# Sparse attention and feed-forward in exact fp32: series and weight conversion in PSUM, chunks of four tiles, the first chunk's strips split around the second chunk

## The chip, the cores and the metric

The kernel runs on one core of a Trainium2 chip. The metric is the time of one execution on the device in microseconds (us), as the median of several runs. The engines are called as in the profile: PE (TensorE matmul), PEld (its weight loads), DVE (VectorE), ACT (ScalarE), POOL (GpSimd), SP (SyncE, which issues the DMAs).

## The reference

Attention over 4 batches of 8 heads, 768 positions, head size 64, with a block mask, and then a feed-forward layer on its output:

```python
scores = scale * q @ k.T                      # (4, 8, 768, 768), blocks of 32
mask = |blk_i - blk_j| <= 1 | first or last block row or column | 3 sampled blocks per row
attn = softmax(where(mask, scores, -1e9));  x = (attn @ v) as 3072 tokens x 512
h = x @ w_in          # 512 -> 2048
g = h - tanh(h)
out = g @ w_out       # 2048 -> 512, fp32
```

`w_in` and `w_out` are float64. q, k, v and the output are fp32.

## The kernel before

**Attention** works on 16 pairs of heads and writes x to DRAM (`xscr`). The change leaves it alone, but for its last rows, which already belong to the feed-forward part.

**Feed-forward** works on tiles of 128 tokens (24 tiles) and on strips of 128 of the 2048 hidden features (16 strips, counted by `ft`). A chunk is a group of tiles that goes through all 16 strips; `CHUNKS` gives chunks of 6 (worked as two halves of 3), 4, 4, 4, 4 and 2 tiles. One step is one strip for one chunk or half:

- `first` (L503): 12 matmuls make `h` of the strip, in a PSUM bank from a pool of two (`one`). Every fp32 product is three matmuls (high by high, high by low, low by high part), over four blocks of 128 features of x.
- The series, which makes `g` = h − tanh(h): ACT makes `u` = h² (L510), `t` = tanh h (L512) and `qq` (L514); POOL a mask `mk` (L516); DVE multiplies out a polynomial for small h in `g` (L518, L520, L521), makes t − h (L519) and copies that over `g` under the mask (L522). All of them but `h` lie in SBUF. Then ACT makes the high part `gh` (L525) and POOL the low part `gl` (L526).
- `second` (L539, L540, L541): three matmuls for each tile add the strip's share to the tile's output bank. Six banks in three tiles of two banks (`big`, named o0, o1, o2) are output banks. After strip 15 they are copied out, by DVE (L545) or ACT (L547), and written by DMA.

`second` of a step is issued two steps after its `first` (`LAG`), so that its series has that long. Where 4 tiles are worked, the next chunk's x is loaded at strip 5 and turned (4 transposes for each tile, L426, into banks 4 and 5, that is tile o2; ACT L428 makes the high part, DVE L429 the low part) from strip 10.

**The weights** come as float64 words. `load_w` brings half a megabyte into one of four `stage` buffers (L400, L404), `convert` makes fp32 from it by three integer operations of DVE (L411, L414, L417, all in SBUF), ACT splits off the high part (L472) and POOL the low part (L474). The six conversions of strips 0 to 2 are done during attention and kept in DRAM; the other 26 lie in the first chunk, two ahead of each strip.

**The order** on each engine is set by a scheduler from the program's order and from the dependencies. It keeps dependencies by tile: two views of one tile, such as the two banks of o2, count as the same, where one of them is written.

Of the kernel before, what the change touches and what calls it, by code (L numbers as in the profile page):

```python
# [406 lines left out]
def convert(nc, pool, raw, name):  # L407

    w = raw.rearrange("p (n w) -> p n w", w=2)
    t = pool.tile([P, 512], I32, tag="wcvt", name=name)  # L410
    nc.vector.tensor_scalar(  # L411
        out=t, in0=w[:, :, 1], scalar1=3, scalar2=0x3FFFFFF8, op0=ALU.logical_shift_left, op1=ALU.bitwise_and
    )
    nc.vector.scalar_tensor_tensor(  # L414
        out=t, in0=w[:, :, 1], scalar=-0x40000000, in1=t, op0=ALU.bitwise_and, op1=ALU.bitwise_or
    )
    nc.vector.scalar_tensor_tensor(  # L417
        out=t, in0=w[:, :, 0], scalar=29, in1=t, op0=ALU.logical_shift_right, op1=ALU.bitwise_or
    )
# [16 lines left out]

class FFN:
    LAG = 2

    def __init__(self, tc, w_in, w_out, xscr, ident, qbias, ps, slots, wt, out, f2):  # L440
        self.nc = tc.nc
        self.tc = tc
        self.w_in, self.w_out, self.xscr, self.ident, self.qbias, self.wt, self.out, self.f2 = (
            w_in, w_out, xscr, ident, qbias, wt, out, f2
        )
# [8 lines left out]
        self.pend = []
        self.raw = {}

    def fetch_w(self, ft):
        nc, tiles, wi, wo, wt = self.nc, self.tiles, self.wi, self.wo, self.wt
        for x, m in enumerate("io"):
            hi, lo = tiles.pop(0), tiles.pop(0)  # L460
            (wi, wo)[x][0][ft], (wi, wo)[x][1][ft] = hi, lo
            if ft < NPRE:
                nc.sync.dma_start(out=lo.bitcast(F32), in_=wt[m, ft])
            else:
                load_w(nc, self.stage[(2 * ft + x) % 4], self.w_in, self.w_out, m, ft)

    def split_w(self, ft):
        nc, wi, wo = self.nc, self.wi, self.wo
        for x, m in enumerate("io"):
            hi, lo = (wi, wo)[x][0][ft], (wi, wo)[x][1][ft]  # L470
            t = lo.bitcast(F32) if ft < NPRE else convert(nc, self.f2, self.stage[(2 * ft + x) % 4], f"cvt{m}{ft}")
            nc.scalar.activation(out=hi, in_=t, func=AF.Copy)  # L472
            eng = nc.vector if ft < 2 and x else nc.gpsimd
            eng.tensor_tensor(out=lo, in0=t, in1=hi.bitcast(F32), op=ALU.subtract)  # L474

    def fetch_x(self, n, j):

        if n == 1:
            raw = self.f2.tile([P, DM], F32, tag="wcvt", name=f"xn{n}_{j}")
        else:  # L480
            raw = self.xbuf[0].bitcast(F32)[:, 4096 + 512 * j : 4096 + 512 * (j + 1)]
        b, t = divmod(self.start[n] + j, T)
# [9 lines left out]
    def first(self, n, s, ft):  # L492
        nc, wi, f2 = self.nc, self.wi, self.f2
        xh, xl = x_parts(self.xbuf[n % 2], sum(CHUNKS[n]))
        t0, nt = sum(CHUNKS[n][:s]), CHUNKS[n][s]
# [4 lines left out]
        for c in range(NCT):  # L500
            cc = slice(c * P, (c + 1) * P)
            for w, x in ((wi[0][ft], xh), (wi[0][ft], xl), (wi[1][ft], xh)):
                nc.tensor.matmul(ph, lhsT=w[:, cc], rhs=x[:, c, tk], start=(k == 0), stop=(k == 3 * NCT - 1))  # L503
# [6 lines left out]
        nc.scalar.activation(out=u, in_=ph, func=AF.Square)  # L510
# [1 line left out]
        nc.scalar.activation(out=t, in_=ph, func=AF.Tanh)  # L512
# [5 lines left out]
        nc.vector.tensor_tensor(out=g, in0=ph, in1=u, op=ALU.mult)  # L518
        nc.vector.tensor_tensor(out=t, in0=t, in1=ph, op=ALU.subtract)  # L519
        nc.vector.scalar_tensor_tensor(out=g, in0=u, scalar=CR, in1=g, op0=ALU.subtract, op1=ALU.mult)  # L520
        nc.vector.scalar_tensor_tensor(out=g, in0=qq, scalar=QC, in1=g, op0=ALU.add, op1=ALU.mult)  # L521
        nc.vector.copy_predicated(g, mk.bitcast(I32), t)  # L522
# [2 lines left out]
        nc.scalar.activation(out=gh, in_=g, func=AF.Copy)  # L525
        nc.gpsimd.tensor_tensor(out=gl, in0=g, in1=gh.bitcast(F32), op=ALU.subtract)  # L526
# [2 lines left out]
    def second(self, n, s, ft, gh, gl):
        nc, wo, f2, out = self.nc, self.wo, self.f2, self.out  # L530
        if not n and not s and not ft:
            big = [self.big(f"o{j}") for j in range(3)]
            self.banks = [x[:, c : c + 512] for x in big for c in (0, 512)]
        banks = self.banks
        t0, nt = sum(CHUNKS[n][:s]), CHUNKS[n][s]
        for j in range(nt):
# [4 lines left out]
            nc.tensor.matmul(o, lhsT=gl[:, c], rhs=wo[0][ft], start=False, stop=(ft == NFT - 1))  # L541
            if ft == NFT - 1:
                ob = f2.tile([P, DM], F32, tag="wcvt", name=f"ob{n}_{t0 + j}")
                if j % 2:
                    nc.vector.tensor_scalar(out=ob, in0=o, scalar1=-1.0, scalar2=None, op0=ALU.mult)  # L545
                else:
                    nc.scalar.activation(out=ob, in_=o, func=AF.Copy, scale=-1.0)  # L547
                b, t = divmod(self.start[n] + t0 + j, T)
                nc.sync.dma_start(out=out[b * S : (b + 1) * S, :].rearrange("(p t) d -> t p d", t=T)[t], in_=ob)

    def step(self):
        n, s, ft = self.units.pop(0)
        if s == 0:
            if n == 0 and ft + 2 < NFT and ft:
                self.split_w(ft + 2)
            if n == 0 and ft and ft + AHEAD < NFT:
                self.fetch_w(ft + AHEAD)
        nx = sum(CHUNKS[n + 1]) if n + 1 < len(CHUNKS) else 0
        if n and ft == 5:
            for j in range(nx):  # L560
                self.fetch_x(n + 1, j)
        if n and 0 <= ft - XF < nx:
            self.turn_x(n + 1, ft - XF)
        self.pend.append((n, s, ft, *self.first(n, s, ft)))
        if n == 0 and ft == NFT - 1:
            js = [j for j in range(nx) if j // 2 == s]
            for j in js:
                self.fetch_x(1, j)
# [56 lines left out]
```

## Time and profile before

| | us |
|---|---|
| Median of 3 runs | 1017.34 (1013.38 to 1064.95) |
| The profiled execution | 1016.33 |
| Its span in the trace | 1014.5 |
| PE busy | 940.8 (93%) |
| DVE busy | 790.6 (78%) |
| POOL busy | 625.4 (62%) |
| ACT busy | 579.3 (57%) |

The span is what the trace covers; 1.8 us of the execution lie around it. `h` of the first feed-forward step starts at 419.15 us, the first chunk goes on to about 608, and the chunks after it have PE busy nearly all the time. Shares of busy time are means over these stages, so the stages are read apart.

### The profile page before, as it was taken

To read this page: it belongs to the slowest core of one execution; us is meant where nothing else is said; L and a number is where in the kernel's file an instruction comes from. 1 tells how busy PE (TensorE), PEld (TensorE's weight loads), DVE (VectorE), ACT (ScalarE), POOL (GpSimd) and SP (SyncE) were. 2 spreads that over 40 slices of the span, in tenths; PEclk is the share of its full clock that TensorE was granted. 3 is DMA by queue.
4 is the path that set the end of the run, shared out by engine and by line. 5 is a ranking of instruction groups with operands and counts; after the bars stand their busy time and mean duration, and the time that the engine had idled before them with its cause. 6 is when DMAs were issued, how large, how long until landed. Compare 5 with 4: busy or idle time off the path is not lost.

```text
span 1014.5 us, 19336 instructions
## 1 busy us (share of the span) xinstructions
PE 940.8 (93%) x7456; PEld 795.6 (78%) x7456; DVE 790.6 (78%) x1194; ACT 579.3 (57%) x912; POOL 625.4 (62%) x436
## 2 busy tenths in 40 slices
PE   5877999999999999986877899999999999999997
PEld 3666888888888887875666788888888888888896
DVE  5799788888888879899999958667666755766676
ACT  1655788888888887643443445444444534444453
POOL 1555687878777878776666646455445544544553
PEclk9798999999999999999989899999999999999999
DMA  7989576667777663143322020011000100000010
GB/s 192 256 226 223 140 187 161 157 173 175 183 168 181 154 147 109 41 159 104 95 92 83 22 94 32 11 32 42 21 11 11 63 1 1 32 11 1 1 42 22
DMA packets 73548, 97.74 MB, mean 96 GB/s; under 512 B 5880, under 2 KB 63416, under 8 KB 73456
## 3 DMA queue, kind: packets, MB, share of 16 engines
q1 hardware_dynamic: 73456, 96.51, 36.1%
q8 instruction: 59, 0.97, 0.4%
q14 instruction: 33, 0.27, 0.1%
HBM read 43.59 MB, written 14.16 MB: 57 GB/s over the span
## 4 chain that ended last, share of the span: by engine, by line
PE 61%; DVE 20%; issue 6%; ACT 5%; DMA 5%; POOL 2%; SPq 1%; POOLq 0%; DVEq 0%; ACTq 0%
PE h L503 21%; PE o L539 7%; PE o L541 7%; PE o L540 7%; PE st L264 4%; PE st L265 4%; PE sm L240 4%; ACT pe L267 2%; DVE mc L241 2%; DVE g L520 2%; PE av L301 2%; PE av L300 2%; PE av L294 2%; DVE g L522 2%; DVE ph L275 1%
## 5 line engine op out<-in xcount | busy, mean ns | idle before, releaser
L279 POOL TENSOR_TENSOR pl<-pe,ph 128x768 f16<-128x768 f32 x173 | 292.0, 1705 | 117.9 <-ACT ph L277 76.7
L526 POOL TENSOR_TENSOR gl<-g,gh 128x512 fp32r<-128x512 f32 (+2 forms) x112 | 132.0, 1181 | 177.3 <-ACT gh L525 176.8
L241 DVE TENSOR_REDUCE mc<-sm 128x1 f32<-128x768 f32 x192 | 180.2, 950 | 39.5 <-PE sm L240 38.6
L516 POOL TENSOR_SCALAR mk<-u 128x512 f32<-128x512 f32 (+2 forms) x112 | 151.5, 1352 | 80.5 <-ACT u L510 42.3
L267 ACT ACTIVATE pe<-st 128x768 f32<-128x768 f32 x192 | 153.5, 803 | 72.6 <-PE st L265 63.1
L525 ACT ACTIVATE gh<-g 128x512 fp32r<-128x512 f32 (+2 forms) x112 | 63.9, 570 | 199.2 <-DVE g L522 190.1
L518 DVE TENSOR_TENSOR g<-h,u 128x512 f32<-128x512 f32 (+2 forms) x112 | 68.4, 611 | 124.5 <-ACT t L512 118.1
L264 PE MATMUL st<-slot 128*128 128x512 f32 (+1 forms) x384 | 144.6, 377 | 7.8 <-DVE mc L241 5.2
L301 PE MATMUL av<-vhl,pl 128*128 128x65 f16 x1152 | 128.6, 194 | 4.8 <-DVE pl L279 3.0
L277 ACT ACTIVATE ph<-pe 128x768 f16<-128x768 f32 x154 | 129.0, 843 | 3.5
L294 PE MATMUL av<-vhl,ph 128*128 128x65 f16 x1152 | 129.1, 195 | 0.5 <-DVE xq L313 0.5
L300 PE MATMUL av<-vhl,ph 128*128 128x64 f16 x1152 | 128.4, 196 | 0.1
L265 PE MATMUL st<-slot 89*128 89x512 f32 (+1 forms) x384 | 125.1, 346 | 2.5 <-DMA slot<-nm 2.5
L503 PE MATMUL h<-slot,wx 128*128 128x384 f32 (+1 forms) x480 | 111.8, 383 | 13.9 <-DVE t L519 13.9
L240 PE MATMUL sm<-slot 88*128 88x512 f32 (+1 forms) x384 | 113.5, 381 | 6.9 <-DMA slot<-hiq 6.3
L301 PEld LDWEIGHTS <-pl 128*128 128x128 f16 x1152 | 107.2, 99 | 15.0 <-issue 5.6
L503 PEld LDWEIGHTS h<-slot,wx 128*128 128x128 f32 x480 | 93.1, 201 | 27.5 <-DVE t L519 17.3
L294 PEld LDWEIGHTS <-ph 128*128 128x128 f16 x1152 | 107.5, 97 | 6.1 <-issue 3.3
L300 PEld LDWEIGHTS <-ph 128*128 128x128 f16 x1152 | 108.4, 98 | 2.3 <-issue 1.9
L510 ACT ACTIVATE u<-h 128x512 f32<-128x512 f32 (+2 forms) x112 | 59.9, 535 | 78.8 <-PE h L503 61.8
L539 PE MATMUL o<-wx,gh 128*128 128x512 f32 x240 | 95.8, 399 | 6.4 <-ACT gh L525 5.4
L521 DVE SCALAR_TENSOR_TENSOR g<-qq,g 128x512 f32<-128x512 f32 (+2 forms) x112 | 89.1, 795 | 8.9 <-DVE g L520 0.5
(101 smaller groups left out, 2008.5 us busy)
## 6 DMA issues: line engine op xcount, KB each, us to landing
slot<-hik SPq DMA_DIRECT2D x64, 192.0 KB
slot<-hiq SPq DMA_DIRECT2D x64, 192.0 KB
stage<-w_in SPq DMA_DIRECT2D x13, 512.0 KB
stage<-w_out SPq DMA_DIRECT2D x13, 512.0 KB
rawk<-k SPq DMA_DIRECT2D x16, 384.0 KB
rawq<-q SPq DMA_DIRECT2D x16, 384.0 KB
slot<-lok SPq DMA_DIRECT2D x32, 192.0 KB
slot<-loq SPq DMA_DIRECT2D x32, 192.0 KB
```

The costliest lines, as they stand in the source:

```text
L240: nc.tensor.matmul(pm[:, c], lhsT=sB[s][0:88, j, t * P : (t + 1) * P], rhs=sA[s][0:88, j, c], start=True, stop=True)
L241: nc.vector.tensor_reduce(out=mcs[h][:, t : t + 1], in_=pm[:, 0:S], op=ALU.max, axis=AX.X)
L264: nc.tensor.matmul(st[:, c], lhsT=sC[s][:, j, kc], rhs=sD[s][:, j, c], start=True, stop=False)
L265: nc.tensor.matmul(st[:, c], lhsT=sA[s][0:89, j, kc], rhs=sB[s][0:89, j, c], start=False, stop=True)
L267: nc.scalar.activation(out=pe, in_=st[:, 0:S], func=AF.Exp, scale=0.125)
L279: d = eng.tensor_tensor(out=pl, in0=pe, in1=ph, op=ALU.subtract)
L294: m = nc.tensor.matmul(o[:, to, :], lhsT=ph[:, c], rhs=vv[:, 0:65], start=(kt == 0 and t == 0), stop=False, skip_group_check=True)
L300: nc.tensor.matmul(o[:, to, 0:64], lhsT=ph[:, c], rhs=vv[:, 65:129], start=False, stop=False, skip_group_check=True)
L301: nc.tensor.matmul(o[:, to, :], lhsT=pl[:, c], rhs=vv[:, 0:65], start=False, stop=last, skip_group_check=True)
L503: nc.tensor.matmul(ph, lhsT=w[:, cc], rhs=x[:, c, tk], start=(k == 0), stop=(k == 3 * NCT - 1))
L516: nc.gpsimd.tensor_scalar(out=mk, in0=u, scalar1=THR2, scalar2=None, op0=ALU.is_gt)
L539: nc.tensor.matmul(o, lhsT=gh[:, c], rhs=wo[0][ft], start=(ft == 0), stop=False)
```

## The change

**The chunks** are all of four tiles. The first chunk's strips are done in two parts: strips 0 to 5, then all 16 strips of the second chunk, then strips 6 to 15 of the first (`SEGS`). The first part's sums are written to DRAM (`part`), read back, and added at the end (L559). Output takes four banks, o0 and o1; there are 96 steps, numbered 0 to 95 below in the order in which they are issued (strip 6 of the first chunk is step 22).

**The series** is kept in PSUM: DVE makes t − h in `t` (L535), then works on `h` in place (L536, L537, L538), and copies it over `t` under a mask (L539). ACT makes the mask (L533, a Relu). GpSimd only makes low parts.

**`h`** goes around in three banks `hb`: the two of `one`, and the left half of o2, which every third step takes (2, 5, 8, ...). **The right half of o2**, `xt`, takes all transposes of x and the in-between results of the weight conversion (L418, L421; L424 reads them and writes to SBUF).

**The conversions** are issued at 1.3 for each step, from step 0 to step 19 (`RATE`). The last four, of strips 14 and 15, pass through a single buffer, `stage1`. The next chunk's x is loaded at strip 8 and turned at strips 10 to 13; the second chunk's at strips 2 to 5 of the first part.

The diff, cut to its core:

```diff
-CHUNKS = ((3, 3), (4,), (4,), (4,), (4,), (2,))
+CT = 4
+SEGS = ((0, 0, 6), (1, 0, 16), (0, 6, 16), (2, 0, 16), (3, 0, 16), (4, 0, 16), (5, 0, 16))
+RATE = 1.3
+NSTAGE, FT1 = 4, 14
...
-def convert(nc, pool, raw, name):
+def convert(nc, pool, raw, name, tmp=None):
     w = raw.rearrange("p (n w) -> p n w", w=2)
     t = pool.tile([P, 512], I32, tag="wcvt", name=name)
+    tmp = t if tmp is None else tmp.bitcast(I32)
...
-        out=t, in0=w[:, :, 1], scalar=-0x40000000, in1=t, op0=ALU.bitwise_and, op1=ALU.bitwise_or
+        out=tmp, in0=w[:, :, 1], scalar=-0x40000000, in1=tmp, op0=ALU.bitwise_and, op1=ALU.bitwise_or
     )
     nc.vector.scalar_tensor_tensor(
-        out=t, in0=w[:, :, 0], scalar=29, in1=t, op0=ALU.logical_shift_right, op1=ALU.bitwise_or
+        out=t, in0=w[:, :, 0], scalar=29, in1=tmp, op0=ALU.logical_shift_right, op1=ALU.bitwise_or
     )
...
     def turn_x(self, n, j):
-        pt = self.banks[4 + j % 2] if n > 1 else self.one(f"xt{n}_{j}")
-        split_x(self.nc, self.raw.pop((n, j)), pt, xh[:, :, jc], xl[:, :, jc], self.ident)
+        split_x(self.nc, self.raw.pop((n, j)), self.xt, xh[:, :, jc], xl[:, :, jc], self.ident)
...
-        ph = self.one(f"h{n}_{s}_{ft}")[:, 0:w_]
+        h = self.hb[self.done % len(self.hb)] if self.hb else self.one(f"h{n}_{ft}")
...
-        nc.gpsimd.tensor_scalar(out=mk, in0=u, scalar1=THR2, scalar2=None, op0=ALU.is_gt)
-        g = tl("g")
-        nc.vector.tensor_tensor(out=g, in0=ph, in1=u, op=ALU.mult)
-        nc.vector.tensor_tensor(out=t, in0=t, in1=ph, op=ALU.subtract)
-        nc.vector.scalar_tensor_tensor(out=g, in0=u, scalar=CR, in1=g, op0=ALU.subtract, op1=ALU.mult)
-        nc.vector.scalar_tensor_tensor(out=g, in0=qq, scalar=QC, in1=g, op0=ALU.add, op1=ALU.mult)
-        nc.vector.copy_predicated(g, mk.bitcast(I32), t)
+        nc.scalar.activation(out=mk, in_=u, func=AF.Relu, scale=-1.0, bias=tbias)
+        nc.vector.tensor_tensor(out=t, in0=t, in1=h, op=ALU.subtract)
+        nc.vector.tensor_tensor(out=h, in0=h, in1=u, op=ALU.mult)
+        nc.vector.scalar_tensor_tensor(out=h, in0=u, scalar=CR, in1=h, op0=ALU.subtract, op1=ALU.mult)
+        nc.vector.scalar_tensor_tensor(out=h, in0=qq, scalar=QC, in1=h, op0=ALU.add, op1=ALU.mult)
+        nc.vector.copy_predicated(t, mk.bitcast(I32), h)
...
+        big = [self.big(f"o{j}") for j in range(3)]
+        self.banks = [x[:, c : c + 512] for x in big[:2] for c in (0, 512)]
+        self.xt = big[2][:, 512:]
+        self.hb = [self.one("hb0"), self.one("hb1"), big[2][:, 0:512]]
...
+        def convert_some(k, end):
+            while k < min(end, math.ceil(RATE * self.done)):
+                self.convert_w(k)
+                if k + NSTAGE < n0:
+                    self.stage_w(k + NSTAGE)
+                elif n0 <= k < n1 - 1:
+                    self.stage_w(k + 1)
+                k += 1
+            return k
```

**Where the instructions stand, DVE.** In the middle of the first chunk of before, DVE's queue mixes the conversion of one weight strip (`cvti9`, `cvto9`) into the series of the half steps (`g0_1_6` is g of chunk 0, half 1, strip 6). The conversion's results go to SBUF, the series reads `h` from banks of its own.

```order
L518 TENSOR_TENSOR g0_1_6_8421<-h0_1_6_8400,u0_1_6_8413 128x384
L519 TENSOR_TENSOR t0_1_6_8415<-t0_1_6_8415,h0_1_6_8400 128x384
L522 COPY_PREDICATED g0_0_6_8381<-mk0_0_6_8379,t0_0_6_8375 128x384
L417 SCALAR_TENSOR_TENSOR cvti9_8440<-stage2_7869,cvti9_8440 128x512
L411 TENSOR_SCALAR cvto9_8446<-stage3_7870 128x512
L520 SCALAR_TENSOR_TENSOR g0_1_6_8421<-u0_1_6_8413,g0_1_6_8421 128x384
L414 SCALAR_TENSOR_TENSOR cvto9_8446<-stage3_7870,cvto9_8446 128x512
L521 SCALAR_TENSOR_TENSOR g0_1_6_8421<-qq0_1_6_8417,g0_1_6_8421 128x384
L417 SCALAR_TENSOR_TENSOR cvto9_8446<-stage3_7870,cvto9_8446 128x512
```

In the changed kernel DVE has this in the second chunk, where `t1_5` is t of chunk 1, strip 5 (step 11, whose `h` lies in o2) and `t1_6` that of the next step:

```order
L424 SCALAR_TENSOR_TENSOR cvti10_8373<-stage2_7855,o2_7847 128x512
L535 TENSOR_TENSOR t1_5_8394<-t1_5_8394,o2_7847 128x512
L536 TENSOR_TENSOR o2_7847<-o2_7847,u1_5_8392 128x512
L535 TENSOR_TENSOR t1_6_8442<-t1_6_8442,hb0_7848 128x512
L536 TENSOR_TENSOR hb0_7848<-hb0_7848,u1_6_8440 128x512
L537 SCALAR_TENSOR_TENSOR o2_7847<-u1_5_8392,o2_7847 128x512
L537 SCALAR_TENSOR_TENSOR hb0_7848<-u1_6_8440,hb0_7848 128x512
L538 SCALAR_TENSOR_TENSOR o2_7847<-qq1_5_8396,o2_7847 128x512
L538 SCALAR_TENSOR_TENSOR hb0_7848<-qq1_6_8444,hb0_7848 128x512
L539 COPY_PREDICATED t1_5_8394<-mk1_5_8398,o2_7847 128x512
L539 COPY_PREDICATED t1_6_8442<-mk1_6_8446,hb0_7848 128x512
L418 TENSOR_SCALAR o2_7847<-stage3_7856 128x512
```

Conversions and every third step's series now name the same tile, o2, and stand in blocks: three or four conversions, then the series of two steps side by side, then conversions again. On PE, the first matmul of step 11 (it writes o2) waits for the row of `cvti10`, and `first` of the step that uses hb0 after strip 6 waits for the row before the last.

**Where the instructions stand, PE.** Before, at strips 11 and 12 of chunk 1, the transposes of chunk 2's x go into o2, which no `first` uses, between matmuls into `h`:

```order
L503 MATMUL h1_0_11_9798<-xbuf1_9100,wx20_7844 128x512 x2
L426 MATMUL o2_7920<-ident_64,slot1_78 128x128 x4
L503 MATMUL h1_0_11_9798<-xbuf1_9100,wx21_7845 128x512
L503 MATMUL h1_0_11_9798<-xbuf1_9100,wx20_7844 128x512 x2
L503 MATMUL h1_0_11_9798<-xbuf1_9100,wx21_7845 128x512
```

Now, at the end of chunk 4, the last turn of chunk 5's x, then strip 13 of chunk 4 and strip 0 of chunk 5 (`slot1`, `slot2`: x and weights of chunk 5's first strip), all in o2:

```order
L433 MATMUL o2_7847<-ident_64,slot1_80 128x128 x4
L553 MATMUL o0_7845<-wx27_7838,gh4_12_11312 128x512
L554 MATMUL o0_7845<-wx26_7837,gl4_12_11313 128x512
L554 MATMUL o1_7846<-wx26_7837,gl4_12_11313 128x512
L552 MATMUL o1_7846<-wx26_7837,gh4_12_11312 128x512
L553 MATMUL o1_7846<-wx27_7838,gh4_12_11312 128x512
L554 MATMUL o1_7846<-wx26_7837,gl4_12_11313 128x512
L520 MATMUL o2_7847<-xbuf1_7843,wx28_7839 128x512 x2
```

The rows go on so, one strip's twelve and then the next strip's:

```order
L520 MATMUL o2_7847<-xbuf1_7843,wx28_7839 128x512 x2
L520 MATMUL o2_7847<-xbuf1_7843,wx29_7840 128x512
L520 MATMUL o2_7847<-slot1_80,slot2_81 128x512 x12
L520 MATMUL hb0_7848<-slot1_80,slot2_81 128x512 x8
L552 MATMUL o0_7845<-wx30_7841,gh4_13_11359 128x512
```

The transposes and two steps' `first` stand close behind each other in one tile, without other matmuls between the two steps. Each waits for the reader of the one before: L520 of strip 13 for DVE's L436 of the turned x, and L520 of strip 0 for L539 of strip 13.

More of the change, by code (lines that the diff above doesn't have):

```diff
@@ L39 @@
 NPRE = 3
-AHEAD = 3
 W0, DW = 40, 24.7
@@ L47 @@
 PB = 8
-XF = 10
+XF = 8
 F0, DF = 12 * (NPAIR - 1) + 1, 2
@@ L80, in attention_ffn @@
     make_identity(nc, ident)
-    qbias = cst.tile([P, 1], F32, name="qbias")
-    nc.vector.memset(qbias, QB)
+    bias = [cst.tile([P, 1], F32, name=f"bias{i}") for i in range(2)]
+    for x, val in zip(bias, (QB, THR2)):
+        nc.vector.memset(x, val)
     big = ctx.enter_context(tc.tile_pool(name="ps_big", bufs=3, space=PSUM))
@@ L91, in attention_ffn @@
     wt = {(m, ft): dpool.tile([P, 512], F32, name=f"w{m}{ft}") for ft in range(NPRE) for m in "io"}
+    part = [dpool.tile([P, DM], F32, name=f"part{j}") for j in range(CT)]
     f2 = ctx.enter_context(tc.tile_pool(name="f2", bufs=2))
-    ffn = FFN(tc, w_in, w_out, xscr, ident, qbias, ps, slots, wt, out, f2)
+    ffn = FFN(tc, w_in, w_out, xscr, ident, bias, ps, slots, wt, out, f2, part)
     with ExitStack() as actx:
@@ L384, in x_first @@
         split_x(nc, raw, pt, xa[0][:, :, j * P : (j + 1) * P], xa[1][:, :, j * P : (j + 1) * P], ident)
-    for j in range(sum(CHUNKS[0])):
+    for j in range(CT):
         at(X0 + DX * j, x_first, j)
@@ L454, in __init__ @@
+        self.done = 0
         self.pend = []
         self.raw = {}
-    def fetch_w(self, ft):
[L458 to L465, printed above, removed]
@@ L467, in split_w @@
-    def split_w(self, ft):
[L468 to L474, printed above, removed]
-    def fetch_x(self, n, j):
[L478 to L482, printed above, removed]
+        self.hb = None
@@ new lines, in place, with parts @@
+    def place(self, m, ft):
+        hi, lo = self.tiles.pop(0), self.tiles.pop(0)
+        w = self.wi if m == "i" else self.wo
+        w[0][ft], w[1][ft] = hi, lo
+        return hi, lo
+    def fetch_w(self, ft):
+        for m in "io":
+            hi, lo = self.place(m, ft)
+            self.nc.sync.dma_start(out=lo.bitcast(F32), in_=self.wt[m, ft])
+    def parts(self, t, hi, lo, eng):
+        self.nc.scalar.activation(out=hi, in_=t, func=AF.Copy)
+        eng.tensor_tensor(out=lo, in0=t, in1=hi.bitcast(F32), op=ALU.subtract)
@@ new lines, in split_w, with stage_w, convert_w @@
+    def split_w(self, ft):
+        for x, w in enumerate((self.wi, self.wo)):
+            hi, lo = w[0][ft], w[1][ft]
+            self.parts(lo.bitcast(F32), hi, lo, self.nc.vector if ft < 2 and x else self.nc.gpsimd)
+    def stage_w(self, k):
+        m, ft = "io"[k % 2], NPRE + k // 2
+        self.raw[m, ft] = self.stage[k % NSTAGE] if ft < FT1 else self.stage1
+        load_w(self.nc, self.raw[m, ft], self.w_in, self.w_out, m, ft)
+    def convert_w(self, k):
+        m, ft = "io"[k % 2], NPRE + k // 2
+        hi, lo = self.place(m, ft)
+        self.parts(convert(self.nc, self.f2, self.raw.pop((m, ft)), f"cvt{m}{ft}", self.xt), hi, lo, self.nc.gpsimd)
@@ L526, in first, with second @@
-        nc.gpsimd.tensor_tensor(out=gl, in0=g, in1=gh.bitcast(F32), op=ALU.subtract)
+        nc.scalar.activation(out=gh, in_=t, func=AF.Copy)
+        nc.gpsimd.tensor_tensor(out=gl, in0=t, in1=gh.bitcast(F32), op=ALU.subtract)
         return gh, gl
[L529 to L536, printed above, removed]
+    def second(self, x, n, ft, gh, gl):
+        nc, wo, f2 = self.nc, self.wo, self.f2
+        _, f0, f1 = SEGS[x]
+        for j in range(CT):
@@ L537, in second @@
             c = slice(j * P, (j + 1) * P)
-            o = banks[t0 + j]
-            nc.tensor.matmul(o, lhsT=gh[:, c], rhs=wo[0][ft], start=(ft == 0), stop=False)
+            o = self.banks[j]
+            nc.tensor.matmul(o, lhsT=gh[:, c], rhs=wo[0][ft], start=(ft == f0), stop=False)
             nc.tensor.matmul(o, lhsT=gh[:, c], rhs=wo[1][ft], start=False, stop=False)
[L541 to L549, printed above, removed]
@@ L551, in step @@
-    def step(self):
[L552 to L568, printed above, removed]
+            nc.tensor.matmul(o, lhsT=gl[:, c], rhs=wo[0][ft], start=False, stop=(ft == f1 - 1))
@@ new lines, in second @@
+            if ft < f1 - 1:
+                continue
+            ob = f2.tile([P, DM], F32, tag="wcvt", name=f"ob{x}_{j}")
+            if f0:
+                nc.vector.scalar_tensor_tensor(
+                    out=ob, in0=o, scalar=-1.0, in1=self.spare[j].bitcast(F32), op0=ALU.mult, op1=ALU.add
+                )
+            elif j % 2:
+                nc.vector.tensor_scalar(out=ob, in0=o, scalar1=-1.0, scalar2=None, op0=ALU.mult)
+            else:
+                nc.scalar.activation(out=ob, in_=o, func=AF.Copy, scale=-1.0)
@@ new lines, in second @@
+            b, t = divmod(CT * n + j, T)
+            if f1 == NFT:
+                nc.sync.dma_start(out=self.out[b * S : (b + 1) * S, :].rearrange("(p t) d -> t p d", t=T)[t], in_=ob)
+            else:
+                nc.sync.dma_start(out=self.part[j], in_=ob)
+                nc.sync.dma_start(out=self.spare[j].bitcast(F32), in_=self.part[j])
+    def step(self):
+        x, n, ft = self.units.pop(0)
+        f0 = SEGS[x][1]
+        last = x == len(SEGS) - 1
+        nx = None if last or x == 1 else {0: 1, 2: 2}.get(x, n + 1)
+        if nx is not None and self.hb:
+            first = 2 if x == 0 else XF
+            if nx == 2:
+                if first <= ft < first + CT:
+                    self.fetch_x(nx, ft - first)
+            elif ft == first:
+                for j in range(CT):
+                    self.fetch_x(nx, j)
+            lag = 0 if x == 0 else 2
+            if 0 <= ft - first - lag < CT:
+                self.turn_x(nx, ft - first - lag)
+        self.pend.append((x, n, ft, *self.first(n, ft)))
+        self.done += 1
@@ L569, in step @@
         if len(self.pend) > self.LAG:
             self.second(*self.pend.pop(0))
-        if n == 0 and ft == NFT - 1:
-            for j in js:
-                self.turn_x(1, j)
     def rest(self, ctx):
-        wc = ctx.enter_context(self.tc.tile_pool(name="wc", bufs=1))
-        self.tiles += [wc.tile([P, 512], F32R, name=f"wx{i}") for i in range(4 * (NFT - 6))]
-        with self.tc.tile_pool(name="stage", bufs=1) as pool:
-            self.stage = [pool.tile([P, 1024], I32, name=f"stage{i}") for i in range(4)]
-            self.fetch_w(AHEAD)
-            while self.units[0][2] < NFT - 2:
+        pool = lambda name: ctx.enter_context(self.tc.tile_pool(name=name, bufs=1))
@@ new lines, in rest @@
+        wc = pool("wc")
+        self.tiles += [wc.tile([P, 512], F32R, name=f"wx{i}") for i in range(4 * (FT1 - 6))]
+        self.xbuf.append(wc.tile([P, 4096], F32R, name="xbuf1"))
+        self.stage1 = wc.tile([P, 1024], I32, name="stage1")
+        big = [self.big(f"o{j}") for j in range(3)]
+        self.banks = [x[:, c : c + 512] for x in big[:2] for c in (0, 512)]
+        self.xt = big[2][:, 512:]
+        self.hb = [self.one("hb0"), self.one("hb1"), big[2][:, 0:512]]
+        n0, n1 = 2 * (FT1 - NPRE), 2 * (NFT - NPRE)
@@ new lines, in rest @@
+        k = 0
+        def convert_some(k, end):
[7 more added lines that the diff above has]
+            return k
+        with self.tc.tile_pool(name="stage", bufs=1) as st:
+            self.stage = [st.tile([P, 1024], I32, name=f"stage{i}") for i in range(NSTAGE)]
+            for i in range(NSTAGE):
+                self.stage_w(i)
+            self.stage_w(n0)
+            while k < n0:
@@ L582, in rest @@
                 self.step()
-        xb = ctx.enter_context(self.tc.tile_pool(name="xb", bufs=1))
-        self.xbuf.append(xb.tile([P, 4096], F32R, name="xbuf1"))
+                k = convert_some(k, n0)
+        wl = pool("wl")
+        self.tiles += [wl.tile([P, 512], F32R, name=f"wy{i}") for i in range(4 * (NFT - FT1))]
         while self.units:
             self.step()
+            k = convert_some(k, n1)
         for p in self.pend:
```

43 lines of the change are left out of this document (22 added, 21 removed).

## The prediction

> **What bounds the kernel now.** I read the profile in stages, since the shares of the page mix two programs. The columns of this view are the stretch, its length, the busy time of PE, PEld, DVE, ACT and POOL (with counts), then the granted clock and the DMA share.
>
> ```profile
> 419.15:608.20 189.05, 157.00 (x765) 133.16 (x766) 171.84 (x248) 81.33 (x161) 120.15 (x92) 0.94 0.28 89
> 608.20:958.50 350.30, 350.30 (x1579) 290.06 (x1578) 228.34 (x341) 158.43 (x278) 177.96 (x127) 1.00 0.06 20
> 958.50:1014.50 56.00, 50.30 (x300) 43.25 (x298) 40.09 (x84) 25.07 (x68) 26.94 (x33) 0.99 0.08 29
> ```
>
> Attention ends at 419.15 and stays as it is. Of the rest, 350.30 us are pure PE (busy 350.30 of 350.30): nothing done for DVE or POOL there can gain. Only the first chunk, with its 26 conversions, leaves PE idle: 32 us of 189.05, with DVE at 171.84. Its waits are for DVE's reader of `h`, since there are two `h` banks (columns: us in total, times, longest):
>
> ```profile
> PE h L503 <- DVE t L519: 20.7, 11, 2.4
> ```
>
> DVE is slow there for a reason that the mean durations show:
>
> ```profile
> L521 DVE SCALAR_TENSOR_TENSOR g<-qq,g 128x384 f32<-128x384 f32 x24 | 28.6, 1192 | 0.4
> L519 DVE TENSOR_TENSOR t<-t,h 128x384 f32<-128x384 f32 x23 | 12.4, 540 | 0.0
> L518 DVE TENSOR_TENSOR g<-h,u 128x512 f32<-128x512 f32 x64 | 44.2, 691 | 109.3 <-ACT t L512 103.8 <-POOL gl L526 5.1
> L520 DVE SCALAR_TENSOR_TENSOR g<-u,g 128x512 f32<-128x512 f32 x64 | 44.6, 697 | 0.0
> ```
>
> At one size, L521 (both inputs in SBUF) takes 1192 ns, where L519 (one input in PSUM) takes 540: the first collides with GpSimd. Later, with GpSimd less loaded, the two kinds cost the same (697 and 691).
>
> **The steady step,** out of chunk 2:
>
> ```profile
> 746.18 2.88 PE L503 MATMUL h<-slot,wx 128*128 128x512 f32 x12
> 748.41 0.63 ACT L525 ACTIVATE gh<-g 128x512 fp32r<-128x512 f32 x1 [2.99 <-DVE g L522]
> 749.12 1.29 POOL L526 TENSOR_TENSOR gl<-g,gh 128x512 fp32r<-128x512 f32 x1 [2.68 <-ACT gh L525]
> 749.16 0.60 ACT L510 ACTIVATE u<-h 128x512 f32<-128x512 f32 x1
> 750.28 0.69 DVE L518 TENSOR_TENSOR g<-h,u 128x512 f32<-128x512 f32 x1 [1.90 <-ACT t L512]
> 750.89 0.68 DVE L519 TENSOR_TENSOR t<-t,h 128x512 f32<-128x512 f32 x1
> 751.48 0.69 DVE L520 SCALAR_TENSOR_TENSOR g<-u,g 128x512 f32<-128x512 f32 x1
> 752.27 0.69 DVE L521 SCALAR_TENSOR_TENSOR g<-qq,g 128x512 f32<-128x512 f32 x1
> 753.07 0.77 DVE L522 COPY_PREDICATED g<-mk,t 128x512 f32<-128x512 int32 x1
> 754.60 0.60 ACT L510 ACTIVATE u<-h 128x512 f32<-128x512 f32 x1
> 641.00:730.00 89.00, 89.00 (x405) 73.59 (x405) 57.68 (x88) 41.02 (x72) 44.40 (x32) 1.00 0.09 30
> ```
>
> A step is 754.60 − 749.16 = 5.44 us, so a `first` or a `second` of four tiles is 2.72. One chunk's 16 steps take 89.00 with its four turned tiles: (89.00 − 87.04) / 4 = 0.49 for each. On DVE operations that don't need the one before start 0.60 apart (750.28, 750.89, 751.48), dependent ones 0.79 (752.27, 753.07). From the end of `first` (746.18 + 2.72) it is 0.26 to `u` and 1.12 more to DVE. So **the series of a step in the new order** (t − h, h·u, two dependent products, the copy) ends 0.26 + 1.12 + 0.60 + 3 × 0.79 + 0.77 = 5.1 us after its `first`; run side by side with another's (ten operations), 0.26 + 1.12 + 9 × 0.60 + 0.77 = 7.5.
>
> **The change, part by part.** *PE's work*: 96 steps × 5.44 + 20 turned tiles × 0.49 = 532.0. Before, 595.35 us from 419.15 on held about the same work, so its waits, half-clock time and tail came to some 63. The forecast is the new list of these.
>
> *What is relieved, without being on the path*: POOL loses the mask; DVE's two-input operations no longer collide. For 24 steps and 26 conversions DVE needs (24 × 5 + 78) × 0.66 = 131 where it now took 171.84. ACT gains a mask of 0.6 for each step, beside 2.6 of 5.44: hidden, as ACT waits for the copy anyway. Partial sums (four tiles out and back) have ten steps until they are needed: hidden by 54 us.
>
> *What is added* is a wait that the order shows: with `h` of every third step, the conversions and the turned x in one tile, o2, `first` waits for a DVE operation that the ring of three alone would not ask for, and behind it PE's whole queue stands still.
>
> (a) **Conversion cycle.** A conversion is L418, L421 and L424; of before:
>
> ```profile
> 433.21 0.62 DVE L411 TENSOR_SCALAR cvti<-stage 128x512 int32<-128x512 int32 x1 [1.30 <-DMA stage<-w_in]
> 434.22 0.68 DVE L414 SCALAR_TENSOR_TENSOR cvti<-stage,cvti 128x512 int32<-128x512 int32 x1
> 435.63 0.68 DVE L417 SCALAR_TENSOR_TENSOR cvti<-stage,cvti 128x512 int32<-128x512 int32 x1
> 428.87 0.40 SPq L400 DMA_DIRECT2D stage<-w_in  x1
> ```
>
> `first` of step 8 can start when cvti8's last operation is done; then DVE does the series of steps 8 and 9 side by side, and `first` of step 12 waits for step 9's copy: 7.5 us with PE idle, as nothing else stands ahead of it. Then five matmul groups follow to the next o2 step. A cycle of three steps is 6 × 2.72 + 7.5 = 23.8. DVE's own 27 operations (some 18 us) with its own idle 4.1 (`first` and the way to DVE) would be 22: not the limit. Three such cycles: 22.5 us of waits. In the fourth, the last three conversions follow each other through one buffer, each with a load of 433.21 − 428.87 = 4.3 and 2.0 on DVE, 19 in a row: I take 14 us of waits in place of 7.5. Step 23 (o2) stands right behind step 20 (o2): 6.9, its copy beside another series.
>
> (b) **Start**, up to step 8. Two series have no cover (4.5 at step 2, whose `second` comes ahead of the next `first`; 7.5 at step 9), and the second chunk's x and the first conversions share the right half: some 13 more, an estimate, since before waited 32 us over this stage. 25 in all; bounds 12 and 32.
>
> (c) **Turns.** A transpose behind an o2 step waits for that step's copy, an o2 step behind a transpose for L436. By the order of PE's rows: chunk 2's turn has two uncovered places (5.1 and 6.9), chunk 3's one (6.9), chunk 4's two half covered (4.2 each), chunk 5's one of 6.9 and one of 1.3; 35.5 us. Before had none (350.30 of 350.30).
>
> (d) **Tail**: before, the last eviction starts at 1010.69 and the span ends at 1014.5, 3.8 later.
>
> ```profile
> 1010.69 0.69 DVE L545 TENSOR_SCALAR ob<-o 128x512 f32<-128x512 f32 x1 [3.62 <-PE o L541]
> ```
>
> Now the last step's four tiles end with some 0.7 of wait for `gl` and the same 3.8: 4.5.
>
> (e) **The clock.** PE's granted clock halves after gaps:
>
> ```profile
> 446.50:448.55 2.05, 0.28 (x2) 0.00 (x1) 2.05 (x5) 1.62 (x3) 1.42 (x2) 1.00 0.35 71
> 449.65:453.05 3.40, 3.40 (x12) 3.11 (x11) 3.40 (x5) 1.45 (x4) 3.40 (x3) 0.50 0.51 161
> ```
>
> 1.8 us of idle PE are followed by 3.4 us at 0.50, that is 1.7 lost where PE is the limit. There are some nine waits of 4 us and more; at 1.5 each, 13.
>
> Sum: 419.15 + 532.0 + 25 + 22.5 + 14 + 6.9 + 35.5 + 4.5 + 13 = 1072.6; with 1.8 around the span 1074.4. The profiled execution of before is 1016.33, 1.0 below the median, so I forecast **1074 us** (5.6% slower).
>
> **What no row shows: DVE writing PSUM.** From below: no operation of 512 columns starts less than 0.60 behind another; if dependent ones in PSUM did so too, the series would be 0.6 shorter, 8 us over a dozen waits: 1066. From above, 0.3 us each (what would bring 0.69 halfway to the slowest row, 1192). I take no change, the nearest row (691 for one that reads PSUM, 697 for one that doesn't). A cost of 0.3 makes the series 0.9 longer at a dozen waits (11) and a conversion cycle, with 14 such writes, 4.2 longer (17): 1103.
>
> [...]
>
> **Rivals.** (1) *The sharing costs nothing*: the waits end before PE gets there, and the relief of DVE comes through. The start takes 12, conversion cycles are DVE's 18 (1.7 over PE's 16.3, four times), the last buffer 10, the tail 4.5, two half-clock stretches 3: 419.15 + 532.0 + 12 + 6.8 + 10 + 4.5 + 3 + 1.8 = 989: faster by 2.7%. It is decided by whether a wait ends within the 5.4 us of two groups that PE could run first; the rows of the order, with an o2 step directly behind an o2 step, speak against it. [...] Chance 0.07. (2) *Waits half covered*: (c) and (e) at half and the start at 12: 1074 − 18 − 6 − 13 = 1037, on the border of 2%. Before's eleven waits of `first` were 2.4 at most, which speaks for it; that those were for banks of tiles of their own speaks against. Chance 0.20. (3) *PSUM writes are dear*: 1103, chance 0.12. (4) *The change doesn't do what it says*, for instance the mask on ACT delays `gh`: 0.6 at each uncovered wait, 8 us more, 1082; inside the forecast's own range.
>
> **Chances and range.** Forecast 0.55 (1050 to 1090), rivals 0.07, 0.20 and 0.12, the rest unforeseen. The range for 8 in 10 takes in (2) and (3): 1034 to 1104. About 2% (997 to 1038) is what can be told from no change: faster 0.07, same 0.13 (over half of (2)), slower 0.80.
>
> **What would show it.** In the changed profile: PE's waits for DVE's L539 and L424 in blocks of about 7 us every 24 us from 495 to 600; at each turn one or two gaps of 4 to 7 us with the clock at 0.50 behind; DVE's L537 near 0.69 without the stretch to 1.1; the first h of step 20 near 597 us. The forecast is wrong if PE is busy without gaps after 610, or if gaps there stay under 2 us.

## The result, and the profile after

| | us | ratio to before |
|---|---|---|
| Before, median | 1016.67 | |
| After, median of 4 runs | 1097.83 (1096.67 to 1100.53) | 1.0814 (1.0777 to 1.085) |
| After, span of the profiled execution | 1094.5 | |

The change makes the kernel 8% slower. One of before's four executions, 1064.95 us, ran in a slower state and is left out of the ratio. The stages of after, in the view of stretches (length, then busy time of PE, PEld, DVE, ACT, POOL, the granted clock, the DMA share):

```profile
419.15:619.20 200.05, 143.77 (x580) 110.23 (x578) 126.06 (x198) 83.64 (x142) 59.39 (x47) 0.86 0.26 81
619.20:1094.50 475.30, 432.61 (x1852) 352.09 (x1852) 267.04 (x401) 229.17 (x396) 97.60 (x76) 0.95 0.07 23
```

In neither stretch is an engine busy all the time. PE idles 56 us in the first and 43 in the second; before had PE idle for 32 us in its first chunk and for none at all from 608 to 958 us. DVE and POOL did get the relief (DVE 126 us, for nearly the work that took 172). The view of waits says whom PE waited for (total, times, longest):

```profile
PE o L520 <- DVE t L539: 24.5, 4, 6.8
PE hb L520 <- DVE t L539: 22.1, 4, 7.3
PE o L433 <- DVE t L539: 17.6, 4, 6.7
PE o L552 <- ACT gh L542: 12.2, 4, 5.1
```

Sixty-four us in twelve waits are for one DVE operation, the copy that ends the series (L539), each up to 7.3 us. One of them, from the timeline of PE and then of DVE, at steps 8 and 12:

```profile
503.10 2.88 PE L520 MATMUL o<-xbuf,slot 128*128 128x512 f32 x12
513.32 1.22 PE L520 MATMUL hb<-xbuf,wx 128*128 128x512 f32 x2 [7.33 <-DVE t L539]
...
507.14 0.69 DVE L535 TENSOR_TENSOR t<-t,o 128x512 f32<-128x512 f32 x1 [6.34 <-ACT t L529]
507.74 0.69 DVE L536 TENSOR_TENSOR o<-o,u 128x512 f32<-128x512 f32 x1
508.34 0.68 DVE L535 TENSOR_TENSOR t<-t,hb 128x512 f32<-128x512 f32 x1
508.94 0.69 DVE L536 TENSOR_TENSOR hb<-hb,u 128x512 f32<-128x512 f32 x1
...
512.54 0.71 DVE L539 COPY_PREDICATED t<-mk,hb 128x512 f32<-128x512 int32 x1
513.15 0.70 DVE L418 TENSOR_SCALAR o<-stage 128x512 int32<-128x512 int32 x1
```

The order of events is to be seen here. PE finishes `first` of step 8 (into o2) at 506; DVE stands idle for 6.34 us, until 507.14, since its next work is on that `h`; then it does the series of both steps side by side, ten operations 0.60 apart; and PE starts again when the tenth is done. The two engines take turns. Right behind that, PE runs at half clock:

```profile
505.99:513.32 7.33, 0.01 (x1) 0.01 (x1) 6.18 (x11) 6.34 (x12) 0.00 (x0) 0.73 0.00 0
513.32:519.50 6.18, 6.18 (x15) 4.88 (x16) 6.02 (x10) 2.32 (x4) 3.81 (x3) 0.50 0.30 87
532.85:540.18 7.33, 0.00 (x1) 0.00 (x0) 6.17 (x11) 6.33 (x12) 0.00 (x0) 0.76 0.00 0
540.18:543.40 3.22, 3.22 (x8) 2.57 (x9) 3.06 (x5) 2.35 (x4) 2.96 (x3) 0.50 0.16 18
866.57:870.79 4.22, 0.00 (x1) 0.01 (x1) 4.22 (x8) 3.27 (x7) 0.00 (x0) 1.00 0.00 0
871.10:874.50 3.40, 3.40 (x11) 2.62 (x9) 1.71 (x4) 2.39 (x5) 2.52 (x2) 0.50 0.28 79
981.66:988.46 6.80, 0.00 (x0) 0.03 (x1) 5.65 (x10) 5.81 (x11) 0.00 (x0) 0.65 0.00 0
988.46:994.00 5.54, 5.54 (x13) 4.38 (x14) 3.32 (x6) 2.29 (x5) 2.53 (x2) 0.50 0.00 0
```

Each pair is a wait and the stretch behind it. Behind a wait of 4.2 us it is 3.4 us of PE at 0.50. Behind waits of about 7 us it is between 3.2 and 6.2, and two waits of the same 7.33 us have the two ends of that range. Over the 17 half-clock stretches after 419 us PE is busy 71 us by the trace's clock records, so some 35 us are lost to the clock; in before it was 23.5 busy and 12 lost.

### The profile page after: what moved, and what is told of

Read it like the earlier page. It is cut to its first block, busy times and chain, and to the rows that moved or that the text cites. A ratio compares the mean times of both kernels' runs of the same rounds, so it can differ in the third digit from the quotient of the medians.

```text
span 1094.5 us, 18614 instructions
## 1 busy us (share of the span) xinstructions
PE 958.9 (88%) x7264; PEld 790.4 (72%) x7264; DVE 745.4 (68%) x1120; ACT 627.1 (57%) x943; POOL 460.7 (42%) x308
## 4 chain that ended last, share of the span: by engine, by line
PE 65%; DVE 17%; ACT 6%; DMA 5%; issue 4%; POOL 1%; SPq 1%; POOLq 0%; DVEq 0%; ACTq 0%
PE hb L520 15%; PE o L520 9%; PE o L552 7%; PE o L553 7%; PE o L554 7%; PE st L270 5%; PE sm L246 4%; PE st L271 4%; ACT pe L273 2%; DVE mc L247 2%; PE av L307 2%; PE av L306 2%; PE av L300 2%; DVE t L535 2%; DVE ph L281 1%
## 5 line engine op out<-in xcount | busy, mean ns | idle before, releaser
L543 POOL TENSOR_TENSOR gl<-t,gh 128x512 fp32r<-128x512 f32 x96 | 123.2, 1289 | 468.6 <-ACT gh L542 418.3
L247 DVE TENSOR_REDUCE mc<-sm 128x1 f32<-128x768 f32 x192 | 180.0, 949 | 36.4 <-PE sm L246 35.5
L542 ACT ACTIVATE gh<-t 128x512 fp32r<-128x512 f32 x96 | 60.3, 628 | 125.8 <-DVE t L539 103.1
L535 DVE TENSOR_TENSOR t<-t,o 128x512 f32<-128x512 f32 x32 | 22.0, 686 | 118.1 <-ACT t L529 118.0
L270 PEld LDWEIGHTS st<-slot 128*128 128x128 f32 x384 | 74.0, 193 | 26.9 <-ACT pe L273 7.5
L535 DVE TENSOR_TENSOR t<-t,hb 128x512 f32<-128x512 f32 x62 | 42.4, 683 | 68.9 <-ACT t L529 68.7
L552 PE MATMUL o<-wx,gh 128*128 128x512 f32 x192 | 77.2, 402 | 5.9 <-ACT gh L542 5.1
L271 PEld LDWEIGHTS st<-slot 89*128 89x128 f32 x384 | 74.5, 194 | 10.1 <-DMA slot<-nm 1.2
L553 PE MATMUL o<-wx,gh 128*128 128x512 f32 x192 | 77.0, 401 | 0.0
L527 ACT ACTIVATE u<-o 128x512 f32<-128x512 f32 x32 | 19.1, 598 | 96.7 <-PE o L520 96.6
```

The costliest lines, as they stand in the source:

```text
L247: nc.vector.tensor_reduce(out=mcs[h][:, t : t + 1], in_=pm[:, 0:S], op=ALU.max, axis=AX.X)
L270: nc.tensor.matmul(st[:, c], lhsT=sC[s][:, j, kc], rhs=sD[s][:, j, c], start=True, stop=False)
L271: nc.tensor.matmul(st[:, c], lhsT=sA[s][0:89, j, kc], rhs=sB[s][0:89, j, c], start=False, stop=True)
```

## The experiments

**1. Is it the shared tile?** o2 becomes two tiles of one bank each; nothing else changes. To make room for tiles of another size, the pool of pairs is closed after attention.

```diff
-        big = [self.big(f"o{j}") for j in range(3)]
-        self.banks = [x[:, c : c + 512] for x in big[:2] for c in (0, 512)]
-        self.xt = big[2][:, 512:]
-        self.hb = [self.one("hb0"), self.one("hb1"), big[2][:, 0:512]]
+        bk = ctx.enter_context(self.tc.tile_pool(name="ps_bank", bufs=1, space=PSUM))
+        big = [bk.tile([P, 1024], F32, name=f"o{j}") for j in range(2)]
+        self.banks = [x[:, c : c + 512] for x in big for c in (0, 512)]
+        self.xt = bk.tile([P, 512], F32, name="xt")
+        self.hb = [self.one("hb0"), self.one("hb1"), bk.tile([P, 512], F32, name="hb2")]
...
```

> The changed kernel with one edit: the two halves of o2 become two PSUM tiles of one bank each (hb2 for h, xt for transposes and conversions); all else as changed. If the waits come from the shared tile, PE's gaps of 4 to 7 us behind it go (61 us of waits at L539 and L424) with the half-clock stretches behind them (some 30): 985 to 1010 us. If the waits come from DVE's own load or from the ring of three, the time stays above 1060.

Measured: 994.61 us (989.79 to 996.75), 0.979 of before (0.9753 to 0.9827). More than 100 us go, and all that is new is that two banks which were halves of one tile are two tiles. In the view of stretches PE is busy all the time where the changed kernel had its turns, and of the twelve waits for L539 one is left:

```profile
640.00:960.00 320.00, 320.00 (x1435) 264.77 (x1434) 209.75 (x311) 177.70 (x306) 75.03 (x58) 1.00 0.06 22
...
PE hb L522 <- DVE t L541: 6.7, 1, 6.7
```

(The lines of this kernel are two further on: L541 is the changed kernel's L539.) So the shared tile is shown as the cause; DVE's load and the ring of three are not it.

**2. The output banks as tiles of their own too.**

```diff
-        big = [bk.tile([P, 1024], F32, name=f"o{j}") for j in range(2)]
-        self.banks = [x[:, c : c + 512] for x in big for c in (0, 512)]
+        bank = lambda name: bk.tile([P, 512], F32, name=name)
+        self.banks = [bank(f"o{j}") for j in range(4)]
...
```

> As the run with o2 cut in two, and the four output banks are tiles of their own too, so that the copy of one output bank no longer holds up matmuls into its neighbour at the end of a chunk. If such pairs matter only there, 5 to 10 us less than with o2 alone cut (seven segment ends, the last one some 3 us); if not, the same within 2 us.

Measured: 988.74 us (985.65 to 990.86), 0.9742 (0.9716 to 0.9768), 6 us less than run 1, as expected of pairs that matter at segment ends. The two intervals overlap by a little, so the waits say it more plainly than the time: run 1 still had 5.3 us of such waits (its row below, PE's L554 for the copy L567), and run 2 has none.

```profile
PE o L554 <- ACT ob L567: 5.3, 3, 3.1
```

This version beats both kernels, by 2.6% and 10%.

**3. The conversions back in SBUF,** o2 still shared by `h` and the transposes.

```diff
-        self.parts(convert(self.nc, self.f2, self.raw.pop((m, ft)), f"cvt{m}{ft}", self.xt), hi, lo, self.nc.gpsimd)
+        self.parts(convert(self.nc, self.f2, self.raw.pop((m, ft)), f"cvt{m}{ft}"), hi, lo, self.nc.gpsimd)
```

> The changed kernel with the in-between results of the conversions in SBUF as before (o2 still shared by h and the transposes). If the shared tile is the cause, the waits from 500 to 620 us go and those at the turns stay: 1097.8 less 35 of waits and some 15 of half clock, 1040 to 1060 us. If DVE's load is the cause, two-input operations that collide with GpSimd again make it no better: 1085 or more.

Measured: 1045.48 us (1042.76 to 1048.83), 1.0305 (1.0275 to 1.0334), inside the 1040 to 1060 expected of the shared tile. Its waits:

```profile
PE o L520 <- DVE t L539: 20.0, 5, 6.8
PE o L433 <- DVE t L539: 17.1, 4, 6.7
PE hb L520 <- DVE t L539: 6.7, 4, 2.3
```

The waits of steps in `hb0` and `hb1`, 22.1 us in the changed kernel, fall to 6.7; those of o2's own steps and of the transposes stay. From 600 us to the tail, PE's gaps of over 1 us are the seven at the turns (4.91, 6.81, 6.71, 4.22, 4.22, 1.28 and 6.80 us). So 52 us of the loss belong to the conversions in the shared tile, and the other 51, against run 1, to the turned x in it.

**4. A bank less.** `h` goes around in two banks, and o2's left half is not used at all.

```diff
-        self.hb = [self.one("hb0"), self.one("hb1"), big[2][:, 0:512]]
+        self.hb = [self.one("hb0"), self.one("hb1")]
```

> The changed kernel with h in the two single banks only; o2's left half is unused, its right half serves conversions and transposes as changed. If the shared tile is the cause, this is faster than the changed kernel though it has a bank less: a step's first then waits for the copy two steps before, which at 5.1 us against 5.44 of cover costs little in the later chunks and some 1 to 2 us a step in the first ones, 1000 to 1030 us. If the depth of the ring matters more, slower than 1098.

Measured: 996.07 us (995.28 to 999.38), 0.9823 (0.9798 to 0.9847), a little under the 1000 to 1030 expected. The third bank, as it was placed, cost 100 us; without it PE waits 13.3 us for copies:

```profile
PE hb L520 <- DVE t L539: 13.3, 4, 4.9
```

This run leaves the pool of pairs as it was, so closing it is not what helped run 1. In a tile of its own (run 1, 994.61) the third bank is worth 1.5 us, less than the intervals tell apart.

**5. Is the rest the clock?** Twenty-six matmuls that add zeros to an output bank stand behind `first` of steps 8, 11, 14, 17 and 20, to keep PE busy in five of the waits.

```diff
+KEEP, NKEEP = (8, 11, 14, 17, 20), 26
...
+        if self.done - 2 in KEEP:
+            for _ in range(NKEEP):
+                m = self.nc.tensor.matmul(self.banks[0], lhsT=self.zero, rhs=self.wi[0][0], start=False, stop=False)
+                self.tc.add_manual_dep(
+                    m.ins, self.ends[self.done - 2].ins.name,
...
```

> The changed kernel, with 26 more matmuls that add zeros to an output bank (5.9 us of PE) right behind the first of steps 8, 11, 14, 17 and 20, that is inside the waits of 5 to 7 us. The half-clock stretches behind these five waits hold 26.5 us of busy PE. If that clock is what the prediction sized too low, they go and the time falls by 10 to 13 us, to 1084 to 1088; if another thing slows the stage, it stays at 1096 to 1101, or grows.

Measured: 1088.8 us (1086.33 to 1090.65), 1.0731 (1.0706 to 1.0757): 9 us less than the changed kernel though PE does 130 matmuls more, a little under the 10 to 13. The stretches of this kernel, then one of the changed one:

```profile
514.07:520.00 5.93, 5.93 (x26) 4.91 (x27) 5.75 (x10) 2.32 (x4) 3.85 (x3) 1.00 0.27 88
489.70:598.90 109.20, 99.32 (x428) 79.22 (x426) 71.92 (x114) 47.13 (x80) 37.22 (x29) 1.00 0.24 78
```

```profile
489.70:598.90 109.20, 80.05 (x303) 63.11 (x302) 69.05 (x109) 46.67 (x79) 36.44 (x29) 0.84 0.24 73
```

In the 6 us behind the first wait PE now does 26 matmuls at clock 1.00, where the changed kernel did 15 at 0.50. The clock's share is shown for these waits; that the same holds at the turns follows from the rows above and was not tried. The gain falls short in part because this kernel has a half-clock stretch that the changed one has not, behind a wait of 2.4 us for a weight (6.44 us of busy PE, 3.2 lost):

```profile
598.92:605.75 6.83, 6.44 (x14) 4.68 (x15) 2.08 (x3) 0.84 (x2) 1.90 (x2) 0.50 0.26 79
```

**6 to 9. What the parts are worth once the tile isn't shared.** Run 6 is run 2 with the polynomial in SBUF, in `g`, as before; `gl` has two buffers for room:

```diff
...
-        nc.vector.tensor_tensor(out=h, in0=h, in1=u, op=ALU.mult)
-        nc.vector.scalar_tensor_tensor(out=h, in0=u, scalar=CR, in1=h, op0=ALU.subtract, op1=ALU.mult)
...
+        nc.vector.tensor_tensor(out=g, in0=h, in1=u, op=ALU.mult)
+        nc.vector.scalar_tensor_tensor(out=g, in0=u, scalar=CR, in1=g, op0=ALU.subtract, op1=ALU.mult)
...
```

> The kernel with all six banks as tiles of their own (988.7), but the polynomial kept in SBUF again (in g, as before; gl has two buffers in place of three to make room). If keeping the series in PSUM is what frees DVE of collisions with GpSimd, its dependent products go from 0.69 to 0.8 or more in the first 200 us and the time to 993 to 1005; if GpSimd is too little loaded to matter once the mask is gone, 987 to 992.

Run 7 is run 2 with the edit of run 3, the conversions in SBUF.

> The kernel with all six banks as tiles of their own (988.7), but the conversions' in-between results in SBUF as before. The bank xt is then for transposes alone, whose one wait of 3.5 us for a conversion goes; DVE's two conversion products read two inputs from SBUF. If collisions with GpSimd are dear, 990 to 996; if they are few, 983 to 988.

Run 8 is the kernel before with the mask on ACT (`self.qbias[1]` holds −THR2):

```diff
-        nc.gpsimd.tensor_scalar(out=mk, in0=u, scalar1=THR2, scalar2=None, op0=ALU.is_gt)
+        nc.scalar.activation(out=mk, in_=u, func=AF.Relu, bias=self.qbias[1])
```

> The kernel before, with the mask made by ACT (a Relu) in place of GpSimd, and nothing else. GpSimd loses 151 us in all, 40 of them in the first chunk, where DVE's two-input products took up to 1.19 us. If the collisions set the first chunk's time, DVE's 172 us there fall by 15 or more and the time to 995 to 1007; if two h banks set it, 1010 to 1017.

Run 9 is run 2 with the mask on GpSimd again:

```diff
-        nc.scalar.activation(out=mk, in_=u, func=AF.Relu, scale=-1.0, bias=tbias)
+        nc.gpsimd.tensor_scalar(out=mk, in0=u, scalar1=THR2, scalar2=None, op0=ALU.is_lt)
```

> The kernel with all six banks as tiles of their own (988.7), with the mask made by GpSimd again (is_lt), the polynomial staying in PSUM. DVE's products read one SBUF input, so they shouldn't collide: if collisions alone made the mask on GpSimd dear, 987 to 993; if GpSimd's own time (1.4 us more a step beside the low parts of the weights) holds up gl, 995 to 1010.

| | us | ratio to before |
|---|---|---|
| 6, series in SBUF | 990.66 | 0.976 (0.9737 to 0.9782) |
| 7, conversions in SBUF | 990.1 | 0.9752 (0.9732 to 0.9772) |
| 8, before, mask on ACT | 999.4 | 0.985 (0.9826 to 0.9874) |
| 9, mask on GpSimd | 988.5 | 0.9756 (0.9725 to 0.9787) |

Runs 6, 7 and 9 can't be told from run 2. In run 6 DVE's two dependent products are dearer in the first stretch (first rows, means 831 and 737 ns) than in run 2 (last rows, 691 and 692):

```profile
L541 DVE SCALAR_TENSOR_TENSOR g<-qq,g 128x512 f32<-128x512 f32 x35 | 28.9, 831 | 0.5
L540 DVE SCALAR_TENSOR_TENSOR g<-u,g 128x512 f32<-128x512 f32 x35 | 25.6, 737 | 0.3
```

```profile
L539 DVE SCALAR_TENSOR_TENSOR hb<-u,hb 128x512 f32<-128x512 f32 x33 | 22.8, 692 | 0.5
L540 DVE SCALAR_TENSOR_TENSOR hb<-qq,hb 128x512 f32<-128x512 f32 x33 | 22.8, 691 | 1.8
```

In run 6 PE waits 12.6 us for `gh`, which is made when the series is done, a wait that run 2 has not:

```profile
PE o L555 <- ACT gh L545: 12.6, 9, 3.9
```

But other waits are shorter by as much: PE's gaps come to 18 us in run 6 and 19 in run 2. In run 7 the conversion's second operation, with both inputs in SBUF, takes 965 to 974 ns against 693 in PSUM. The 990 to 996 expected for dear collisions begins at run 7's 990.1, and the time can't show them.

Run 8, one operation moved in the kernel before, gives 14 us. Its dearest product, first before and then in run 8:

```profile
L521 DVE SCALAR_TENSOR_TENSOR g<-qq,g 128x384 f32<-128x384 f32 x32 | 34.9, 1091 | 0.5
```

```profile
L523 DVE SCALAR_TENSOR_TENSOR g<-qq,g 128x384 f32<-128x384 f32 x32 | 23.4, 731 | 0.4
```

DVE is busy 155 us in the first chunk (419 to 590 us) in place of 172. PE's waits for t − h, the last reader of `h`, fall from the 20.7 us of the kernel before to 9.9, while those for GpSimd's `gl` grow from 2.9 to 10.7:

```profile
PE o L543 <- POOL gl L528: 10.7, 8, 1.5
PE h L505 <- DVE t L521: 9.9, 11, 1.4
```

The clock has a share in the gain: after 419 us PE is busy 3.4 us at half clock in run 8, against 23.5 before, so some 10 of the 18 us between the two profiled executions come from there. In before's first chunk nine of the 32 L521 ran with no GpSimd operation beside them and took 540 to 559 ns; the others took up to 1652. L519, with one input in PSUM, took 532 to 547 with and without one. All of this fits collisions as what made the first chunk of before long; a GpSimd that is as busy without collisions was not tried.

So in the new chunks neither part is needed while the other stays: the mask off GpSimd is enough (run 6), and so are the products out of SBUF (run 9). A kernel with neither was not tried, so what the two bring together is not known, and no run splits the 2.6% of run 2 between the chunks, the mask and the ring.

**10. Conversions earlier.** Run 2 with `RATE = 1.7` in place of 1.3.

> The kernel with all six banks as tiles of their own (988.7), with 1.7 conversions for each step in place of 1.3. If the start's waits (5.5 us for the first converted strip, 6.1 for a copy) come from the conversions' lateness, 983 to 987; if DVE is what is short there, conversions ahead of the series make it 990 to 996.

Measured: 983.86 us (982.83 to 988.63), 0.9713 (0.9682 to 0.9744). That is the lowest median, but its interval overlaps with run 2's, which was measured at another time: a gain is likely and not shown.

## Why the prediction was right, and what it sized wrong

The forecast of slower held, and the time, 1097.83, lies in the range of 1034 to 1104, 24 us above the point. It lies outside the narrower 1050 to 1090 that the forecast gave itself, and near the third rival's 1103, whose mechanism the runs rule out. Step by step:

- **The mechanism** was right: PE waits for L539 through o2, shown by runs 1, 3 and 4.
- **The waits, place by place** (each is the gap before the waiting row in PE's timeline): conversion cycles 7.5 forecast, 7.33, 7.33 and 6.65 measured; step 23 6.9, measured 6.71; turns 5.1, 6.9, 6.9, 4.2, 4.2, 1.3 and 6.9 forecast, 5.36, 6.80, 6.71, 4.22, 4.22, 1.28 and 6.80 measured, 35.5 against 35.4 in all. The way to get them, a series' latency from start-to-start times of the steady step, can be trusted. Two estimates were high: the start (25; gaps of 16.5, without the 3.0 us wait for the end of attention) and the fourth cycle (14, gaps of 7.6).
- **The clock was the term that was sized wrong**: (e) took 13 us, and some 35 were lost. It took 1.5 us for each of nine waits, from before's short gaps, which are followed by one stretch of 3.4 us. Eleven waits of 4.2 to 7.3 us are followed by 3.2 to 6.2 us of busy PE at 0.50, a loss of 2.4 us each on average, and the start has five stretches of its own, 8.5 us lost, which the sum left out.
- **Luck**: this term's miss, 22 us, equals the whole miss of the span (1072.6 forecast, 1094.5 measured) only because the other errors cancel. The waits of the list were forecast 16 us too long; 7 us of waits that the list hasn't (the end of attention, weights, the tail) and some 9 us of PE work beyond the 532.0, which I can't assign (the ends of matmuls are modelled), make up for it.
- **A sign that missed**: `h` of step 20 was forecast near 597 us and starts at 609.46, behind the `h` of steps 22 and 21, which PE does first.
- **Tail and rates**: 3.8 us from last eviction to the end (1090.69 to 1094.5), as forecast; the pairs o0 and o1 added 1.77 of wait before it, which was not foreseen.
- **DVE writing PSUM** cost nothing here, as taken: 0.69 in the timeline above, means of 692 to 696 ns in the changed kernel's groups that write it (L418, L421, L536 to L538), against before's 697 with both inputs in SBUF. The bound from below didn't come about either: L538 starts 0.80 us behind L537, and L539 0.80 behind L538 (medians of those that stand next to each other), where before's L521 starts 0.79 behind L520. Its 0.60 holds within the series alone: before's L417 starts at 435.63 us, 0.32 behind L411, both of 512 columns. The third rival falls with the measured rows.
- **The first rival** had the right price for a kernel in which the sharing costs nothing: 989 worked out, 988.74 in run 2, where the output pairs are cut as well (994.61 in run 1, with o2 alone). Its terms agree less well: it put 17 us of waits into conversion cycles and the last buffer, where run 2 has no gap over 0.3 us after 488 us, and took 12 for the start and 3 for the clock, which were 19 and 8.

## What to carry to other kernels

This program's scheduler keeps a dependency by the tile, not by the bank: two things of different rhythm in one tile are chained even where they never touch, and an extra buffer that is half of a shared tile can be worse than none (run 4: 996.07 us against 1097.83). Read the waits from the built order before trusting a ring's depth, and give each ring member a tile of its own. Price a wait of PE with its clock: here a gap of 4.2 to 7.3 us cost another 1.6 to 3.1 behind it.

## What the runs showed of the hardware that I had not expected

Filler matmuls that do nothing else (run 5) bought 9 us (1088.8 against 1097.83). In run 5 gaps of up to 1.44 us behind the filler brought no half clock (1.00 from 489.70 to 598.90 us), while in the kernel before 1.78 us did. The length of a gap alone doesn't decide it here. In the clock records of the traces of before and of the changed kernel the stretches at 0.50 (11 and 19) begin, in each trace, on one grid of 3.413 us and, but for the one at the program's end, last one to three steps of it (3.413, 6.827 or 10.24 us). From 420 us on in the two traces, at full clock, all 307 steps of the grid in which PE idled for less than 0.50 of it were followed by full clock, all 20 with more than 0.56 by half, and of the 6 between five by half; at half clock, full clock came back after all 23 steps with no more than 0.12 idle and after none of the 13 with more than 0.17. So in before a gap of 1.78 us inside one step was followed by half clock (first two rows), and one of 2.42 us, from 479.41 to 481.83, which lies across two steps, was not (last two rows):

```profile
446.23:449.64 3.41, 1.63 (x9) 1.21 (x8) 3.41 (x7) 2.07 (x5) 2.16 (x3) 1.00 0.53 154
449.64:453.05 3.41, 3.41 (x12) 3.12 (x11) 3.41 (x5) 1.46 (x4) 3.41 (x3) 0.50 0.51 161
476.95:480.36 3.41, 1.80 (x8) 0.91 (x6) 3.41 (x5) 0.98 (x2) 2.41 (x2) 1.00 0.43 141
480.36:483.78 3.42, 1.95 (x11) 1.95 (x12) 3.42 (x7) 1.66 (x4) 2.28 (x2) 1.00 0.10 17
```

The same grid tells the two waits of 7.33 us apart: PE starts again at 513.32, 0.60 us into a step, and stays at half for that step and the next; at 540.18 it starts 0.16 us into one, and is at full clock after it.
